# Strassen quads for q and k of four head groups in a fused attention and gMLP kernel, with the first score gather moved ahead of the v gathers

## The chip, the cores and the metric

One NeuronCore of one Trainium2 chip runs the whole program. The metric is device time in microseconds (us), the median over several executions. A profile of one execution gives the span from the first to the last instruction, a few us shorter than the device time. Engines: PE is TensorE, DVE is VectorE, ACT is ScalarE, POOL is GpSimd, SP is the engine that issues most DMAs. "L435" is line 435 of a kernel's source; the change adds lines, so L293 of the kernel before is L294 of the changed one, and L1405 is L1478.

## The reference, cut to what matters

```python
# x: (1, 2048, 1024); 32 heads of 32; a query sees 8 keys, 2 positions apart
q, k, v = split(x @ wqkv)
logits  = where(mask, q . k[pos - 2*w], -1e9)          # w = 0..7
a       = (softmax(logits) . v[pos - 2*w]) @ wo
z       = gelu(x @ w_in);  z1, z2 = halves(z);  z2 = layernorm(z2)
b       = (z1 * (w_sp @ z2 + b_sp)) @ w_out
out     = g * a + (1 - g) * b                          # g = sigmoid(sum(x * gate_w))
```

The kernel handles attention in eight groups of four heads. For one group, q and k are 256 output columns, from a contraction of 1024 over 2048 tokens. Done directly, that is 2 x 4 x 8 = 64 matmuls of 512 columns.

## The kernel before: the parts that matter

TensorE runs the stages in this order: v and q/k of the first groups; then for each group the q and k of the next group, with three sets of small banded score matmuls between; in the middle the rest of v; then z2, z1, the spatial product and the output. The attention of a group (maxima, exponential, weights, products with v) runs on VectorE and ScalarE behind it, and lasts far into the z1 stage. One Python scheduler estimates each engine's clock and hands VectorE a piece of attention when it believes that there is room.

q and k are direct:

```python
def qk_tile(g, t, c, bank=low_bank):              # t: q or k; c: 512 tokens
    ps = bank()
    for kt in range(KT):                          # 8
        nc.tensor.matmul(ps[:], w[:, t, kt, :], xT[:, kt, 512*c:512*(c+1)], ...)
    act(0.5, pe(T_QK) + 0.2)
    nc.scalar.copy(dst[:, :, 256*c:256*(c+1)], ...)
```

v, z2 and z1 are already Strassen quads: a 2 x 2 block product by seven block products rather than eight, in four PSUM banks. Each block product is four matmuls. In z2 and z1 the sums of the outputs are made by accumulating on copied "seeds" and by two adds on VectorE (`plus`, L506 in the profile); v uses a variant with seed copies alone (L453, L464 and L477, on ScalarE). The form with adds is this one:

```python
def chain(A11, ..., S1..S4, B11, ..., T1..T4, vs, put, share, N, ...):
    X, Y, Z, V = bank_roles[side]
    product(X, A11*B11);  nc.scalar.copy(Y, X)     # seed, L518    ; yield
    product(V, S1*T1);    share(vs, V)             # share, L524   ; yield
    product(Y += S2*T2);  plus(Z, Y)     # VectorE: Z = Y + vs     ; yield
    product(X += A12*B21); put(0, 0, X)                           ; yield
    product(Y += S3*T3);  plus(V, Y);  put(1, 1, V)               ; yield
    product(Z += S4*B22); put(0, 1, Z)                            ; yield
    product(Y or X += A22*T4); put(1, 0, ...)                     ; yield
# (condensed: clock bookkeeping and the copy that only non-lean quads make are cut)
```

Two quads normally run in turn, in the lower and the upper four banks, so that one quad's copies and adds hide behind the other's products. The S sums are sums of weights (VectorE, L577), the T sums are sums of x, made once. `mark` is a short matmul over a bank that a quad is to accumulate into. The Trainium skill ("PSUM — Partial Sum Buffer", section "The four PSUM rules") says why it is needed: a matmul that begins an accumulation clears the written bits of the whole bank, in the 32-partition quadrants that it writes, and an element whose bit is clear is overwritten where it should be added to. The band scores clear those of the upper banks.

The order of the first gathers, where `next_v` issues two v gathers of 960 KB each:

```python
    clock["SP"], clock["DMA"] = 4.0, 4.0
    next_v()                     # v of groups 0 and 1
    load_wqk_later(3, 0.0)       # weights of group 3
    # the gather of the first scores is issued only behind these
```

## Time and profile before

| | before |
|---|---|
| device time at the prediction | 663.26 us (662.23 to 663.37, 3 runs) |
| span of the profile | 657.9 us, granted clock 1.000 |
| PE busy | 650.5 us, 99% |
| VectorE busy | 503.2 us, 76% |
| ScalarE busy | 290.0 us, 44% |

First the page of the kernel before: span, busy time by engine, VectorE's busy tenths in 40 slices, and three of its groups of instructions (busy time, mean ns of one, then the idle time before them and what ended it).

```profile
span 657.9 us, 11379 instructions
PE 650.5 (99%) x4453; PEld 341.3 (52%) x4453; DVE 503.2 (76%) x762; ACT 290.0 (44%) x632; POOL 6.2 (1%) x15
DVE  2520889978999999898778676887659999595952
...
L435 PE MATMUL psum_all<-arena 128*128 128x512 f16 (+6 forms) x2238 | 442.0, 360 | 0.7 <-DVE psum_all L506 0.6
L293 PE MATMUL psum_all<-arena 128*128 128x512 bf16 x512 | 114.8, 379 | 0.0
...
L506 DVE TENSOR_TENSOR psum_all<-psum_all,arena 128x448 f32<-128x448 f32 (+1 forms) x58 | 37.2, 660 | 4.5 <-PE psum_all L435 3.6
```

PE is the bound: it waits for almost nothing, so only fewer matmuls can shorten the program. The 379 ns of one matmul is its latency, and the matmuls overlap; the chain of waits has 1314 matmuls of 512 columns in 283.7 us, 0.216 us each. This agrees with the Trainium skill ("TensorE: Matmul & The Clock Gate", section "Wait — 56ns, not 53.3ns?": 215.7 ns). L293 counts the direct 512-column matmuls, which the change halves. VectorE is at 80% or more in 23 of the 36 slices from 66 us on, so whatever is added there may turn into a wait of PE. One slack is visible: the first score maximum waits until 64.7 us for its gather. From VectorE's timeline, before (start, duration, instruction, and in brackets the idle time before it and what ended it):

```profile
64.70 0.29 DVE L671 TENSOR_TENSOR att_m<-att_L 128x256 f16<-128x256 f16 x1 [16.96 <-DMA att_L<-band_d]
```

### The profile page before, as it was taken

To read this page: it belongs to the slowest core of one execution; us is meant where nothing else is said; L and a number is where in the kernel's file an instruction comes from. 1 tells how busy PE (TensorE), PEld (TensorE's weight loads), DVE (VectorE), ACT (ScalarE), POOL (GpSimd) and SP (SyncE) were. 2 spreads that over 40 slices of the span, in tenths; PEclk is the share of its full clock that TensorE was granted. 3 is DMA by queue.
4 is the path that set the end of the run, shared out by engine and by line. 5 is a ranking of instruction groups with operands and counts; after the bars stand their busy time and mean duration, and the time that the engine had idled before them with its cause. 6 is when DMAs were issued, how large, how long until landed. Compare 5 with 4: busy or idle time off the path is not lost.

```text
span 657.9 us, 11379 instructions
## 1 busy us (share of the span) xinstructions
PE 650.5 (99%) x4453; PEld 341.3 (52%) x4453; DVE 503.2 (76%) x762; ACT 290.0 (44%) x632; POOL 6.2 (1%) x15
## 2 busy tenths in 40 slices
PE   8999999999999999999999999999999999999998
PEld 4544467444454555444444444444444444868684
DVE  2520889978999999898778676887659999595952
ACT  4544676555588677799654112111121112202120
POOL 1000000000000000001000000000000000000000
PEclk9999999999999999999999999999999999999999
DMA  9988554797586050249974568559697463455501
GB/s 217 189 212 225 124 129 122 176 222 188 120 213 179 1 156 1 65 129 249 248 205 159 121 171 166 143 157 280 127 186 172 97 153 91 117 136 115 134 19 56
DMA packets 230198, 98.20 MB, mean 149 GB/s; under 512 B 177520, under 2 KB 217088, under 8 KB 230144
## 3 DMA queue, kind: packets, MB, share of 16 engines
q1 hardware_dynamic: 229856, 97.27, 61.2%
q8 instruction: 35, 0.57, 0.4%
q10 hardware_dynamic: 288, 0.20, 0.1%
q14 instruction: 19, 0.16, 0.1%
HBM read 45.10 MB, written 36.61 MB: 124 GB/s over the span
## 4 chain that ended last, share of the span: by engine, by line
PE 95%; ACT 2%; DMA 2%; DVE 1%; issue 0%; SPq 0%; DVEq 0%; ACTq 0%
PE psum_all L435 66%; PE psum_all L293 17%; PE psum_all L1391 7%; PE psum_all L303 3%; PE psum_all L355 2%; DMA arena<-o_d 1%; DMA arena<-in_A_x_dram 1%; ACT arena L815 1%; ACT arena L363 0%; SPq L162 0%; PE psum_all L822 0%; DVE arena L708 0%; DVE psum_all L506 0%; ACT L815 0%; PE psum_all L225 0%
## 5 line engine op out<-in xcount | busy, mean ns | idle before, releaser
L435 PE MATMUL psum_all<-arena 128*128 128x512 f16 (+6 forms) x2238 | 442.0, 360 | 0.7 <-DVE psum_all L506 0.6
L435 PEld LDWEIGHTS <-arena 128*128 128x128 f16 (+1 forms) x2238 | 218.8, 98 | 222.2 <-issue 2.2
L293 PE MATMUL psum_all<-arena 128*128 128x512 bf16 x512 | 114.8, 379 | 0.0
L293 PEld LDWEIGHTS <-arena 128*128 128x128 bf16 x512 | 48.4, 98 | 56.2 <-issue 0.2
L708 DVE TENSOR_TENSOR arena<-arena,att_A 128x2048 f16<-128x2048 bf16 (+1 forms) x44 | 73.3, 1703 | 0.3
L296 ACT CAST arena<-psum_all 128x512 bf16<-128x512 f32 x64 | 37.2, 585 | 51.2 <-PE psum_all L293 51.2
L1391 PE MATMUL psum_all<-arena 128*128 128x256 f16 (+1 forms) x468 | 51.9, 273 | 1.0 <-DVE psum_all L1405 1.0
L1391 PEld LDWEIGHTS <-arena 128*128 128x128 f16 x468 | 45.8, 98 | 6.8 <-issue 1.3
L815 ACT ACTIVATE arena<-psum_all 128x448 bf16<-128x448 f32 x64 | 34.1, 545 | 18.8 <-DVE psum_all L506 9.2
L453 ACT COPY psum_all<-psum_all 128x512 f32<-128x512 f32 (+1 forms) x24 | 12.4, 517 | 67.4 <-PE psum_all L435 66.6
L506 DVE TENSOR_TENSOR psum_all<-psum_all,arena 128x448 f32<-128x448 f32 (+1 forms) x58 | 37.2, 660 | 4.5 <-PE psum_all L435 3.6
L1095 ACT ACTIVATE arena<-psum_all 128x512 bf16<-128x512 f32 x56 | 31.5, 600 | 21.0 <-PE psum_all L435 13.9
L712 DVE TENSOR_TENSOR arena<-arena 128x2048 f16<-128x2048 f16 (+1 forms) x22 | 37.1, 1704 | 0.1
L363 ACT CAST arena<-psum_all 128x1988 f16<-128x1988 f32 (+3 forms) x25 | 33.9, 1356 | 1.1 <-PE psum_all L355 0.3
L870 ACT ACTIVATE arena<-arena 128x896 bf16<-128x896 bf16 x32 | 30.4, 958 | 0.0
L477 ACT COPY psum_all<-psum_all 128x512 f32<-128x512 f32 (+1 forms) x24 | 12.4, 518 | 37.0 <-PE psum_all L435 36.0
L581 DVE TENSOR_TENSOR arena<-arena 128x1024 f16<-128x1024 f16 (+2 forms) x17 | 12.2, 720 | 19.5 <-PE psum_all L435 15.7
L464 ACT COPY psum_all<-psum_all 128x512 f32<-128x512 f32 (+1 forms) x24 | 12.4, 518 | 25.6 <-PE psum_all L435 24.8
L459 ACT COPY arena<-psum_all 128x512 f32<-128x512 f32 (+1 forms) x24 | 12.7, 532 | 24.9 <-PE psum_all L435 22.5
L303 PE MATMUL psum_all<-arena 128*128 128x385 bf16 x128 | 22.6, 327 | 0.0
L671 DVE TENSOR_TENSOR att_m<-att_L 128x256 f16<-128x256 f16 x8 | 2.3, 288 | 23.8 <-DMA att_L<-band_d 23.8
L713 DVE TENSOR_TENSOR arena<-arena 128x2048 f16<-128x2048 f16 x16 | 19.5, 1221 | 0.3
(111 smaller groups left out, 510.9 us busy)
## 6 DMA issues: line engine op xcount, KB each, us to landing
arena<-v_d SPq DMA_DIRECT2D x8, 960.0 KB, 5.9
z_d<-arena SPq DMA_DIRECT2D x14, 512.0 KB, 4.7
arena<-z_d SPq DMA_DIRECT2D x14, 512.0 KB, 4.3
zg_d<-arena SPq DMA_DIRECT2D x56, 128.0 KB, 2.2
arena<-zg_d SPq DMA_DIRECT2D x32, 224.0 KB, 3.2
band_d<-arena SPq DMA_DIRECT2D x28, 248.5 KB, 4.4
arena<-in_A_wqkv_dram SPq DMA_DIRECT2D x16, 256.0 KB, 5.0
o_d<-arena SPq DMA_DIRECT2D x4, 1024.0 KB, 5.8
```

Of the source, the lines that this page charges most:

```text
L293: nc.tensor.matmul(ps[:], w[:, t, kt, :], xT[:, kt, 512 * c:512 * (c + 1)], start=(kt == 0), stop=(kt == KT - 1))
L296: nc.scalar.copy(dst[:, :, 256 * c:256 * (c + 1)], ps[:].rearrange("p (n e) -> p e n", e=2))
L303: nc.tensor.matmul(ps[:, 0:VP + 1], xT[:, kt, i * P:(i + 1) * P], wvp[:, kt, :], start=(kt == 0), stop=(kt == KT - 1))
L363: nc.scalar.copy(dst, src)
L435: nc.tensor.matmul(bank[:, 0:N], lhsT, rhs, start=(start and m == 0), stop=(m == n - 1), skip_group_check=True)
L506: last_add[0] = nc.vector.tensor_tensor(out[:, n], a[:, n], vs, ALU.add)
L708: lambda ws=ws, in0=in0, in1=in1: tt(p5[:, ws], in0[:, ws], in1[:, ws], ALU.mult)), False
L712: lambda a=p3[:, ws], b=p3[:, ws.start + 4:ws.stop + 4]: tt(a, a, b, ALU.add)), not n
L815: nc.scalar.activation(z2[:, i + 8 * a, ZC * c:ZC * (c + 1)], bank[:, 0:ZC], ACT.Gelu_apprx_tanh, accum_out=s1[:, 4 * n + c:4 * n + c + 1])
L870: return nc.scalar.activation(junk, src, ACT.Square, accum_out=(s2, s2h)[x][:, n:n + 1])
L1095: last_gelu[0] = nc.scalar.activation(z1s[:, f, a, :], bank[:], ACT.Gelu_apprx_tanh)
L1391: nc.tensor.matmul(bank[:, h], l, r, start=(start and m == 0), stop=(m == len(ab) - 1), skip_group_check=True)
```

## The change

q and k of groups 2 to 5 become two quads per group: 2 x 7 x 4 = 56 matmuls rather than 64. There is one quad per 512-token chunk of the two token halves. Two of the four quads of a pair of groups can run beside each other; the others run alone in the lower banks, while a group's band scores use the upper ones. The first score gather goes to the head of the queue, so that VectorE can start attention earlier, to pay for the new adds.

```diff
+    PAIRS, FINE_TO = (2, 4), -1
+    def qk_sums(g):                      # four 128x512 sums of weights, VectorE
+    def qk_quad(g, c, side):
+        def put(t, x, bank):
+            act(0.5, max(clock["PE"], clock["DVE"] if t + x == 2 else 0.0) + 0.2)
+            nc.scalar.copy((qT_slots, kT_slots)[t][g % 2][...], bank[:]...)
+        return chain(..., qv_slots[side], put, nc.scalar.copy, 512, side=side, lean=True, done=done)
+    BAND_AT = (1, 3, 6)
+    def among_bands(g, quad):            # one quad alone, band sets behind its products 1, 3, 6
+        for n in range(7):
+            next(quad); step()
+            if n + 1 in BAND_AT:
+                band_set(g, x); x += 1; step()
+    def play_group(g):
+        if g + 1 in PAIRS:
+            among_bands(g, qk_quad(g + 1, 0, 0))
+            first = qk_quad(g + 1, 1, 0)
+            ... two products of it ...
+            mark(bank_roles[1][1:3], 512)
+            run(qk_quad(g + 2, 0, 1), first, step=step)
+        elif g in PAIRS:
+            among_bands(g, qk_quad(g + 1, 1, 0))
...
-    clock["SP"], clock["DMA"] = 4.0, 4.0
+    clock["SP"], clock["DMA"] = 5.5, 5.5
+    next_bands()                         # first score gather
+    dma(0.0, 0.1, lambda: sync.dma_start(g_att[:], ...))
+    next_v(1)
+    load_wqk_later(3, 0.0)
     next_v()
-    load_wqk_later(3, 0.0)
...
-        z1s, vs = z1s_slots[fp in (2, 4)][c], zv_slots[c]
+        z1s, vs = z1s_slots[fp == 3][c], zv_slots[c]
...
-        ... vs, gelu, share, 512, lean=True, done=store)
+        ... vs, gelu, nc.scalar.copy if not fp else share, 512, lean=True, done=store)
```

(`FINE_TO = -1` also splits the first of VectorE's products with v, of groups 0 to 4, into quarters of 1.2 us.)

More of the change, by code (lines that the diff above doesn't have):

```diff
@@ L140 @@
     wqk_slots = [z2[:, 8 * (r % 2):8 * (r % 2) + 8, 896 * (r // 2):896 * (r // 2) + 256].rearrange("p k (t c) -> p t k c", t=2) for r in range(4)]
-    wqk_slots += wqk_slots[0:2] + [reg(R_OFF + 34752 + 2048 * r, 2048).rearrange("p (k t c) -> p t k c", k=KT, t=2) for r in (0, 1)]
+    wqk_slots += wqk_slots
     wvp = z2[:, 0:KT, ZC:ZC + VP + 1]
@@ L409 @@
     sync.dma_start(bass.AP(tensor=g_d.tensor, offset=g_d.offset, ap=[[P, 16], [1, P]]), g_s[:])
-    sync.dma_start(bass.AP(tensor=og_d.tensor, offset=og_d.offset, ap=[[P, 16], [1, P]]), omg_h[:])
-    gate_dma = sync.dma_start(g_att[:], bass.AP(tensor=g_d.tensor, offset=g_d.offset, ap=[[NJ, P], [1, NJ]]))
+    gate_dma = sync.dma_start(bass.AP(tensor=og_d.tensor, offset=og_d.offset, ap=[[P, 16], [1, P]]), omg_h[:])
     def x_sums(r):
@@ L723, in products @@
             next_v()
-    SPLIT, FINE = [[slice(n * x, n * x + n) for x in range(8 // n)] for n in (4, 2)], 4
+    SPLIT, FINE = [[slice(n * x, n * x + n) for x in range(8 // n)] for n in (4, 2)], FINE_TO
     sent = []
@@ L728, with next_v @@
     bands_at, bands_have = [0], [0]
-    def next_v():
-        while v_at[0] < min(v_have[0], gone[0] + 2):
+    def next_v(upto=NG):
+        while v_at[0] < min(v_have[0], gone[0] + 2, upto):
             h = v_at[0]
@@ L875 @@
     quads = [(0, i) for i in range(7)] + [(1, i) for i in range(8)]
+    QSET = [g + x for g in PAIRS for x in range(2)]
+    qs_slots = [z2h[:, 0:16, 256 + 896 * r:384 + 896 * r].rearrange("p (q k) c -> p q k c", q=4) for r in range(2)]
+    qv_slots = [reg(R_OFF + 34752 + 1024 * r, 1024).bitcast(F32) for r in range(2)]
+    q_landed, q_free = {}, [int(2 in PAIRS), 0]
+    def qk_sums(g):
+        w, s = wqk_slots[g], qs_slots[g % 2]
+        return sums4_steps([s[:, q] for q in range(4)], w[:, 0, 0:4], w[:, 0, 4:8], w[:, 1, 0:4], w[:, 1, 4:8])
@@ new lines, in qk_push, with qk_ready, done @@
+    def qk_push(r):
+        while q_free[r] == 0 and q_landed.get(r):
+            g, t = q_landed[r].pop(0)
+            q_free[r] = 1
+            fill.extend((t, 0.34, f) for f in qk_sums(g))
+    def qk_ready(g, t):
+        q_landed.setdefault(g % 2, []).append((g, t + LATE))
+        qk_push(g % 2)
+    def qk_quad(g, c, side):
+        w, s = wqk_slots[g], qs_slots[g % 2]
+        a, b = w[:, 0], w[:, 1]
+        lo, hi = slice(512 * c, 512 * c + 512), slice(1024 + 512 * c, 1536 + 512 * c)
+        def put(t, x, bank):
+            act(0.5, max(clock["PE"], clock["DVE"] if t + x == 2 else 0.0) + 0.2)
+            nc.scalar.copy((qT_slots, kT_slots)[t][g % 2][:, :, 256 * (c + 2 * x):256 * (c + 2 * x + 1)], bank[:].rearrange("p (n e) -> p e n", e=2))
+        def done():
+            if c == 1:
+                q_free[g % 2] = 0
+                qk_push(g % 2)
+        return chain([a[:, k] for k in K4], [a[:, 4 + k] for k in K4], [b[:, 4 + k] for k in K4],
+                     *[[s[:, q, k, :] for k in K4] for q in range(4)],
+                     [xT[:, k, lo] for k in K4], [xT[:, 4 + k, lo] for k in K4], [xT[:, 4 + k, hi] for k in K4],
+                     *[[x[:, k, lo] for k in K4] for x in xts], qv_slots[side], put, nc.scalar.copy, 512, side=side, lean=True, done=done)
@@ new lines @@
+    BAND_AT = (1, 3, 6)
+    def among_bands(g, quad):
+        x = 0
+        for n in range(7):
+            next(quad)
+            step()
+            if n + 1 in BAND_AT:
+                band_set(g, x)
+                x += 1
+                step()
+        bands_have[0] = g + 1
+        next(quad, 0)
+    def play_group(g):
+        if g + 1 in PAIRS:
+            among_bands(g, qk_quad(g + 1, 0, 0))
+            first = qk_quad(g + 1, 1, 0)
+            for _ in range(2):
+                next(first)
+                step()
+            mark(bank_roles[1][1:3], 512)
+            run(qk_quad(g + 2, 0, 1), first, step=step)
+        elif g in PAIRS:
+            among_bands(g, qk_quad(g + 1, 1, 0))
+        else:
+            return False
+        return True
@@ L912, in step @@
         advance(clock["PE"])
-    def behind_first(n):
-        at = [0]
-        def f():
-            at[0] += 1
-            if at[0] == 1:
-                mark(banks[5:7], n)
-            step()
-        return f
     def play(items):
@@ L939, in load_wqk_later @@
     def load_wqk_later(g, at):
-        dma(at, 2.9, lambda: load_wqk(g, sync.dma_start))
+        dma(at, 2.9, lambda: load_wqk(g, sync.dma_start), (lambda t: qk_ready(g, t)) if g in QSET else None)
     settle()
@@ L948 @@
     band_data[0], band_free[0], v_data[0] = T_START
-    clock["SP"], clock["DMA"] = 4.0, 4.0
+    clock["SP"], clock["DMA"] = 5.5, 5.5
     stored.clear()
     bands_have[0] = 1
+    next_bands()
+    dma(0.0, 0.1, lambda: sync.dma_start(g_att[:], bass.AP(tensor=g_d.tensor, offset=g_d.offset, ap=[[NJ, P], [1, NJ]])))
+    next_v(1)
+    load_wqk_later(3, 0.0)
     next_v()
-    load_wqk_later(3, 0.0)
+    if 2 in PAIRS:
+        fill.extend((1.5, 0.34, f) for f in qk_sums(2))
     for g in range(NG):
@@ L958 @@
         hold[0] = g == NG - 1
-        play(main[0:8 - (not g)])
+        paired = play_group(g)
+        if not paired:
+            play(main[0:8 - (not g)])
         if g == 2:
-            for i in range(0, 8, 2):
-                run(v_quad(i), v_quad(i + 1), step=behind_first(VH) if i == 0 else step)
+            first = v_quad(0)
+            for _ in range(3):
+                next(first)
+                step()
+            mark(bank_roles[1][1:3], VH)
+            run(v_quad(1), first, step=step)
+            for i in range(2, 8, 2):
+                run(v_quad(i), v_quad(i + 1), step=step)
             advance(clock["PE"] + 1.0)
@@ L966 @@
             load_later(0, clock["PE"] + 4.0, 6.0)
-        play(main[8 - (not g):])
+        if not paired:
+            play(main[8 - (not g):])
     load_later(1, clock["PE"] + 3.0, 2.0)
@@ L984, in quad_step @@
             if n == 0 and count[0] == 0:
-                mark(banks[5:7], ZC)
+                mark(bank_roles[1][1:3], ZC)
             step()
@@ L1103, in z1_quad @@
                      [xT[:, k, lo] for k in K4], [xT[:, 4 + k, lo] for k in K4], [xT[:, 4 + k, hi] for k in K4],
-                     *[[x[:, k, lo] for k in K4] for x in xts], vs, gelu, share, 512, lean=True, done=store)
+                     *[[x[:, k, lo] for k in K4] for x in xts], vs, gelu, nc.scalar.copy if not fp else share, 512, lean=True, done=store)
     z1_junk = free(BC_OFF, FH)
@@ L1123 @@
     dma(clock["PE"] + 1.0, 2.9, lambda: load_w1(1), w1_landed(1))
+    RAW_IN = 3.0
+    DRAIN, SUMS = 1, NFH - 2
     RAW_AT = {2: {2: 0, 4: 1, 6: 2}, 3: {4: 3, 6: 4}, 4: {2: 5, 4: 6, 6: 7}}
@@ L1129 @@
             w1_sums(fp + 1)
-        if fp == NFH - 2:
-            fill.extend((clock["PE"] + 3.0, 1.15, f) for f in wsp_sums(0, 0))
+        if fp == SUMS:
+            fill.extend((clock["PE"] + RAW_IN, 1.15, f) for f in wsp_sums(0, 0))
         late = () if fp else [b[2] for b in bank_roles]
@@ L1135 @@
             step=lambda: z1_step(fp, at))
-        if fp == 1:
+        if fp == DRAIN:
             drain()
```

## The prediction

> **What bounds the kernel now.** TensorE. The engine table has PE busy 650.5 us of 657.9 (99%); the chain of waits is 95% PE, at a granted clock of 1.00. A 512-column matmul costs 0.216 us in the chain (1314 in 283.7 us), as the Trainium skill has it ("TensorE: Matmul & The Clock Gate", section "Wait — 56ns, not 53.3ns?": 215.7 ns). VectorE is second: by stretches it is busy 77.5 of 81.2 us in the z2 stage (191 to 272) and 22.4 of 24.4 us in the first two z1 passes (272.2 to 296.6). Its attention work ends at 294.7, only 2 us before the second z1 pass.
>
> **Removed.** q and k of a group are 64 matmuls of 512 columns; as two quads 2x7x4 = 56. Four groups save 32. Each pair of groups needs two marking matmuls, which set the written bits of banks that the band scores cleared: 4 added. Net 28 x 0.216 = 6.05 us of TensorE, all on the chain. Two VectorE copies of the first z1 pass (0.69 each) go to ScalarE.
>
> **Added on VectorE.** 16 PSUM adds of 512 columns, 0.65 each in sequence: 10.4 us. Weight sums of groups 3 to 5: 12 x 0.43 = 5.1 (those of group 2 fall into the idle 17 us before 64.7). Attention products of groups 0 to 4 in quarters: 1.9. Less the two copies: 16 us net before attention ends.
>
> **Added on ScalarE.** 16 seed and share copies, 9 us; it is 66% busy there and off the chain, except where a 1.8 us band eviction sits between a product and its share copy.
>
> **Moved.** The first score gather is issued at 57.0 behind two v gathers and a weight load, and lands at 64.7. Going first, it can land near 58.5: VectorE starts 6 us earlier. Its waits for the scores of groups 4 and 5 (2.5 + 1.4 + 2.7 us between 142 and 160) also fill up.
>
> **On the critical path.** 6.05 us of TensorE less new waits. (a) A single quad has no partner: a product two steps later needs the VectorE add, covered by one product and one band set, 0.86 + 0.6 us. An attention piece of 1.2 us in the way costs some tenths: 1 us over four single quads. (b) VectorE, with 16 us more and 12 us of room gained, ends attention at 296 to 298, while TensorE ends the second z1 pass near 291.5. The third pass can run 4 to 5 us before it needs an add queued behind attention. So 1 to 3 us of stall. The rest of z1 has 11 us of VectorE slack, so little is lost before the spatial stage. Estimate: 663.3 - 6.05 + 1 + 2 = 660.2 us.
>
> **Predicted:** 660.2 us, 656.8 to 664.0. Faster by over 2%: 0.01; within 2%: 0.97; slower by over 2%: 0.02.
>
> **What would show it.** Direct 512-column bf16 matmuls fall from 512 to 256, quad matmuls rise by 224. First score maximum near 58 to 60, not 64.7. Between 60 and 185 PE has waits of tenths on VectorE adds. A PE wait of 1 to 3 us on a VectorE add near 295. The spatial stage starts 3 to 5 us before 357.1; after that both run alike. ScalarE plus 9 us, VectorE plus 16 us busy in all.
>
> **What would make it wrong.** VectorE's lag absorbed: all 6 us gained (657). VectorE lagging longer: spatial weights load late behind the attention's store, another stall before the spatial stage, no gain or a loss. Late weights for group 3 stalling the first paired quads.

## The result, and the profile after

Ratios in this document are of fast runs alone, with a 95% interval. They are not quite the ratios of the medians that are quoted, nor of the plain means of all runs listed (for e12 the means give 0.9993).

| chip | before, median | changed, median | ratio |
|---|---|---|---|
| first | 663.32 us (4 runs) | 660.64 us (4 runs, 660.34 to 662.54) | 0.9969 [0.9948, 0.9991] |
| second (run e2_after) | 660.80 us (7 runs) | 658.46 us (4 runs) | 0.9957 [0.9938, 0.9976] |
| third (run e9_after) | 661.83 us (11 runs) | 659.29 us (6 runs) | 0.9969 [0.9953, 0.9986] |

The gain is 2.3 to 2.7 us on three chips, less than half of one per cent. From the page of the changed kernel:

```profile
span 660.7 us, 11409 instructions
PE 647.5 (98%) x4425; PEld 339.9 (51%) x4425; DVE 518.8 (79%) x822; ACT 298.1 (45%) x650; POOL 6.5 (1%) x15
DVE  2534989998799999999888666987669999594952
...
L435 PE MATMUL psum_all<-arena 128*128 128x512 f16 (+6 forms) x2462 | 494.8, 362 | 4.0 <-DVE psum_all L506 2.7
L294 PE MATMUL psum_all<-arena 128*128 128x512 bf16 x256 | 57.5, 379 | 0.0
L506 DVE TENSOR_TENSOR psum_all<-psum_all,arena 128x512 f32<-128x512 f32 (+1 forms) x74 | 48.0, 668 | 4.6 <-PE psum_all L435 2.5
```

The counts are as intended: 512 direct matmuls became 256, and L435 has 224 more. VectorE has 15.6 us more and ScalarE 8.1 us. New in this page is the last column of L435: those matmuls waited 4.0 us in all, not 0.7. The first score maximum comes 7.6 us earlier (VectorE's timeline, changed kernel):

```profile
57.13 0.29 DVE L671 TENSOR_TENSOR att_m<-att_L 128x256 f16<-128x256 f16 x1 [7.90 <-DMA att_L<-band_d]
```

The profiled run on the first chip was the slowest of its four (662.54 us), and the run profiled before took 659.77 us, less than any of the four in the table (662.23 to 663.42). The two profiles can't be subtracted. The second chip gives a clean pair, one profile of each kernel, both at full clock (spans of 659.2 and 657.0 us). This table cuts them at the same points of the program; the output stage begins with its first seed copy on ScalarE, and the table ends with the start of VectorE's last add.

| stretch | before (e1_before) | changed (e2_after) | difference |
|---|---|---|---|
| start to the q/k tiles behind v | 44.49 | 44.88 | +0.39 |
| q/k, bands and v, to the first z2 tile | 137.87 | 133.27 | -4.60 |
| z2 | 91.40 | 91.69 | +0.29 |
| z1 and spatial | 288.02 | 288.79 | +0.77 |
| output | 94.42 | 95.24 | +0.82 |
| sum | 656.20 | 653.87 | -2.33 |

The +0.39 lies ahead of anything that was changed. To see where the rest goes, take all waits of PE between 60 and 640 us of that changed run (the other fields as above; a line can hold many matmuls, and its wait is that before the first):

```profile
89.27 0.70 PE L435 MATMUL psum_all<-arena 128*128 128x320 f16 x4 [0.94 <-ACT psum_all L453]
184.34 0.64 PE L356 MATMUL psum_all<-arena 32*64 32x71 bf16 x56 [0.31 <-ACT arena L364]
195.52 13.78 PE L435 MATMUL psum_all<-arena 128*128 128x448 f16 x72 [2.49 <-DVE psum_all L506]
209.46 60.55 PE L435 MATMUL psum_all<-arena 128*128 128x448 bf16 x316 [0.16 <-DVE psum_all L506]
326.08 231.97 PE L435 MATMUL psum_all<-arena 128*128 128x512 f16 x1074 [0.71 <-DVE psum_all L506]
572.55 4.09 PE L1464 MATMUL psum_all<-arena 128*128 128x256 f16 x36 [1.40 <-DVE psum_all L1478]
```

The same kernel before had these in the z2 stage (PE's timeline of e1_before):

```profile
198.45 10.75 PE L435 MATMUL psum_all<-arena 128*128 128x448 f16 x56 [1.20 <-DVE psum_all L506]
210.37 4.89 PE L435 MATMUL psum_all<-arena 128*128 128x448 f16 x25 [1.17 <-DVE psum_all L506]
```

Four things can be read here.

First, the q/k stretch became 4.60 us shorter with a new wait of 0.94 us in it, so 5.54 us of work went; the prediction had 6.05. The other half microsecond is in the starts of single matmuls. The matmul that waits starts 1.24 us after the one before it, where 0.14 is usual, so the wait cost 1.10 us and not 0.94; and two others, at 95.38 and 128.28 us, keep the next one waiting 0.17 us longer than their like. The wait stands where the first v quads begin, right behind the last single quad. ScalarE, which works its queue in order, had this ahead of the seed copy L453 (ScalarE's timeline, e2_after):

```profile
86.56 1.83 ACT L364 CAST arena<-psum_all 128x1988 f16<-128x1988 f32 x1
88.27 0.62 ACT L903 CAST arena<-psum_all 128x512 bf16<-128x512 f32 x1
88.75 0.47 ACT L453 COPY psum_all<-psum_all 128x320 f32<-128x320 f32 x1
```

The eviction of the last band set (1.83 us) and one of the quad's own evictions (0.62 us) come first, and PE starts when the seed is there. No wait in the single quads themselves is on a VectorE add.

Second, at the start of z2 PE waits 2.49 us for a VectorE add. VectorE's timeline just ahead of that add (e2_after):

```profile
186.45 4.63 DVE L708 TENSOR_TENSOR arena<-arena,att_A 128x2048 f16<-128x2048 bf16 x4
191.11 0.29 DVE L692 TENSOR_TENSOR att_A<-att_L,att_r 128x256 f16<-128x256 f16 x1
191.31 2.35 DVE L712 TENSOR_TENSOR arena<-arena 128x2048 f16<-128x2048 f16 x2
193.70 1.22 DVE L713 TENSOR_TENSOR arena<-arena 128x2048 f16<-128x2048 f16 x1
194.84 1.16 DVE L506 TENSOR_TENSOR psum_all<-psum_all,arena 128x448 f32<-128x448 f32 x2
```

Eight pieces of attention, 8.4 us from 186.45 to 194.84, stand ahead of the first two adds of z2. The Trainium skill ("Perfetto Trace Analysis", section "Per-engine timelines") calls VectorE and ScalarE strict FIFO, and this agrees: no add passes a piece. But the kernel before lost 1.20 + 1.17 us at the same stage, so most of this wait isn't new on this pair of runs; in the first profile of before it was 0.59 us.

Third, in the third z1 pass PE waits 0.71 us at 326. VectorE had waited there for a weight load (`in_B_w_in`) that before was not late. The load was issued at 312.66 us, about when it was in e1_before (312.91), though TensorE had begun z1 3.92 us earlier; in both it follows a group of transposing weight loads and two z1 stores in the DMA queue. Fourth, the output stage loses 0.9 us more to the load of the attention output (1.40 us, where before had 0.20 and 0.27).

On the first chip three of the changed kernel's four runs also had a mean granted clock of 0.997. The stretch right behind the z2 wait shows why (windows of 4 us, first chip's changed profile: after the busy times comes the granted clock, then DMA share and GB/s):

```profile
192.00:196.00 4.00, 2.19 (x12) 1.02 (x11) 3.93 (x6) 3.49 (x8) 0.00 (x0) 1.00 0.98 283
196.00:200.00 4.00, 3.43 (x13) 1.58 (x13) 3.96 (x7) 0.53 (x2) 0.00 (x0) 0.72 1.21 210
200.00:204.00 4.00, 4.00 (x20) 1.90 (x18) 3.93 (x6) 3.27 (x13) 0.00 (x0) 0.85 1.03 242
```

PE's wait there was 2.38 us. The clock was then 0.72 and 0.85, which is (0.28 + 0.15) x 4 = 1.72 us of work not done. The Trainium skill ("TensorE: Matmul & The Clock Gate", section "Part 1: The HAM clock gate") has a gate that falls to half speed after an idle window of about 3.4 us, in windows that run free. Half speed for one such window is an estimated 1.7 us. The trace agrees on the half and on the length (same profile, the stretch of the dip alone):

```profile
197.80:201.21 3.41, 3.41 (x11) 1.36 (x9) 3.41 (x5) 1.69 (x6) 0.00 (x0) 0.50 1.19 162
```

It differs on how much idleness that takes. The clock changes in each trace lie on steps of 3.41 us, counted from the first rise of the clock (6.65 us here; 197.80 is 56 steps later). The dips of one step came behind steps that held 2.18 us of a PE wait (here), 2.17 (e10), 2.52 (e12) and 3.08 us (e7). No step with 1.79 us or less had a dip behind it. The waits of 2.49 us in e2_after and 2.35 us in e9_after were cut in two by a step's end (1.70 + 0.79 and 1.64 + 0.71), and no dip followed. "PE busy" hides this loss, since a slower matmul counts as busy. The times of the runs do not show it, though: on the first chip the one run at full clock took 660.81 us, and two of the three at 0.997 took 660.34 and 660.48.

### The profile page after: what moved, and what is told of

It reads as the page before. It is cut to its first block, busy times and chain, and to the rows that moved or that the text cites. A ratio compares the mean times of both kernels' runs of the same rounds, so it can differ in the third digit from the quotient of the medians.

```text
span 660.7 us, 11409 instructions
## 1 busy us (share of the span) xinstructions
PE 647.5 (98%) x4425; PEld 339.9 (51%) x4425; DVE 518.8 (79%) x822; ACT 298.1 (45%) x650; POOL 6.5 (1%) x15
## 4 chain that ended last, share of the span: by engine, by line
PE 81%; DVE 9%; DMA 6%; ACT 1%; issue 1%; SPq 1%; DVEq 0%; ACTq 0%
PE psum_all L435 64%; PE psum_all L1464 7%; PE psum_all L294 5%; PE psum_all L304 3%; DMA band_d<-arena 2%; DMA arena<-o_d 1%; DVE arena L708 1%; PE psum_all L356 1%; DMA arena<-in_B_w_in_dram 1%; SPq L190 1%; DVE arena L1247 1%; DVE arena L712 1%; DVE arena L577 1%; PE psum_all L319 1%; ACT arena L815 0%
## 5 line engine op out<-in xcount | busy, mean ns | idle before, releaser
L435 PE MATMUL psum_all<-arena 128*128 128x512 f16 (+6 forms) x2462 | 494.8, 362 | 4.0 <-DVE psum_all L506 2.7
L435 PEld LDWEIGHTS <-arena 128*128 128x128 f16 (+1 forms) x2462 | 240.2, 98 | 251.0 <-issue 8.0
L708 DVE TENSOR_TENSOR arena<-arena,att_A 128x2048 f16<-128x2048 bf16 x64 | 75.3, 1219 | 0.3
L294 PE MATMUL psum_all<-arena 128*128 128x512 bf16 x256 | 57.5, 379 | 0.0
L506 DVE TENSOR_TENSOR psum_all<-psum_all,arena 128x512 f32<-128x512 f32 (+1 forms) x74 | 48.0, 668 | 4.6 <-PE psum_all L435 2.5
L453 ACT COPY psum_all<-psum_all 128x512 f32<-128x512 f32 (+1 forms) x24 | 12.5, 519 | 67.2 <-PE psum_all L435 66.4
L294 PEld LDWEIGHTS <-arena 128*128 128x128 bf16 x256 | 24.4, 98 | 28.4 <-issue 0.2
L712 DVE TENSOR_TENSOR arena<-arena 128x2048 f16<-128x2048 f16 x32 | 38.1, 1218 | 0.0
L477 ACT COPY psum_all<-psum_all 128x512 f32<-128x512 f32 (+1 forms) x24 | 12.4, 518 | 37.4 <-PE psum_all L435 36.6
L297 ACT CAST arena<-psum_all 128x512 bf16<-128x512 f32 x32 | 18.6, 587 | 23.2 <-PE psum_all L294 23.0
L577 DVE TENSOR_TENSOR arena<-arena 128x512 f16<-128x512 bf16 (+3 forms) x52 | 25.2, 522 | 3.0 <-DMA arena<-in_B_w_in_dram 2.6
L464 ACT COPY psum_all<-psum_all 128x512 f32<-128x512 f32 (+1 forms) x24 | 12.4, 518 | 25.9 <-PE psum_all L435 25.1
L518 ACT COPY psum_all<-psum_all 128x512 f32<-128x512 f32 (+1 forms) x37 | 20.4, 562 | 6.3 <-PE psum_all L435 5.5
```

The lines of the kernel that those rows point to most:

```text
L294: nc.tensor.matmul(ps[:], w[:, t, kt, :], xT[:, kt, 512 * c:512 * (c + 1)], start=(kt == 0), stop=(kt == KT - 1))
L435: nc.tensor.matmul(bank[:, 0:N], lhsT, rhs, start=(start and m == 0), stop=(m == n - 1), skip_group_check=True)
L506: last_add[0] = nc.vector.tensor_tensor(out[:, n], a[:, n], vs, ALU.add)
L577: return [lambda a=a: nc.vector.tensor_tensor(*a) for a in args]
L708: lambda ws=ws, in0=in0, in1=in1: tt(p5[:, ws], in0[:, ws], in1[:, ws], ALU.mult)), False
L712: lambda a=p3[:, ws], b=p3[:, ws.start + 4:ws.stop + 4]: tt(a, a, b, ALU.add)), not n
```

## The experiments

Twelve kernels were run. Runs of one chip share their runs of before, so ratios are safer than medians. One run of e5 was slow (clock 0.655) and is left out of its ratio.

| run | chip | median us | before on that chip | ratio |
|---|---|---|---|---|
| e1_before | second | 660.34 | 660.80 | 0.9994 [0.9979, 1.0009] |
| e2_after | second | 658.46 | 660.80 | 0.9957 [0.9938, 0.9976] |
| e3_order_only | second | 663.23 | 660.80 | 1.0039 [1.0020, 1.0057] |
| e4_pairs_only | second | 668.73 | 660.80 | 1.0118 [1.0091, 1.0145] |
| e5_order_pure | fourth | 663.53 | 661.31 | 1.0029 [1.0014, 1.0044] |
| e6_z1slots | fourth | 660.96 | 661.31 | 0.9997 [0.9982, 1.0012] |
| e7_lag_known | fourth | 660.35 | 661.31 | 1.0006 [0.9980, 1.0032] |
| e8_band_early | fourth | 661.53 | 661.31 | 1.0011 [0.9998, 1.0023] |
| e9_after | third | 659.29 | 661.83 | 0.9969 [0.9953, 0.9986] |
| e10_qk_pool | third | 664.50 | 661.83 | 1.0057 [1.0034, 1.0079] |
| e11_qk_wz_pool | third | 688.73 | 661.83 | 1.0413 [1.0395, 1.0431] |
| e12_no_sums | fifth | 660.28 | 660.64 | 0.9989 [0.9976, 1.0003] |

All but e12 were correct; e12 is wrong. The changed kernel itself wasn't run on the fourth and fifth chips, so a comparison of e6, e7, e8 and e12 with it goes over two chips, through before. Their ratios are all near 1.000, so it isn't excluded that the change is worth less on those two chips. Their profiles show TensorE's part of the gain there too: the q/k stretch took 133.27 us in e7 and 133.38 in e12, as in e2 (133.27). No variant's ratio was better than that of the change.

### e1_before and e2_after: both kernels again

No edit.

> The kernel before, unchanged, once more: for the spread of its times, clocks and profiles. Both theories: 662 to 664 us, ratio 1.000. The first profile was a lucky run (659.8 against a median of 663.3); if the difference is a slowed clock after a TensorE wait in the z2 stage, this one's clock is below 1.000 in the slower runs.

> The changed kernel once more. 660 to 661 us. Theory A (VectorE runs behind and stalls TensorE): the 2.4 us wait on the VectorE add at the start of the z2 stage and the slowed clock behind it are there again. If the wait was chance, it is not.

The kernel before against itself gives 0.9994, with an interval of 0.0015 on each side, so differences of two or three parts in a thousand can be seen. The gain holds (0.9957). e1's times (660.05 to 661.05 us) lie below the 662 to 664 that were expected, and its slowest run was at full clock, so a slowed clock isn't what sets the runs of before apart. In e2 the expected wait at z2 came again (2.49 us), the slowed clock behind it did not. The table by stretches comes from this pair.

### e3_order_only and e4_pairs_only: one part of the change each

e3 keeps the reordered gathers and the z1 changes, without quads. e4 keeps the quads, with the old order of the first gathers.

```diff
# e3, against the changed kernel
-    PAIRS, FINE_TO = (2, 4), -1
+    PAIRS, FINE_TO = (), 4
# e4, against the changed kernel
-    clock["SP"], clock["DMA"] = 5.5, 5.5
+    clock["SP"], clock["DMA"] = 4.0, 4.0
-    next_bands()
-    ... next_v(1)
+    next_v()
     load_wqk_later(3, 0.0)
-    next_v()
```

> The change without the quads for q and k and without the finer attention products: only the earlier score gather, and the small changes in z1. Theory A: VectorE starts attention 7 us earlier, and the kernel before lost about 2 to 3 us to waits on it, so 660 to 663 us. Theory B (the order is worth nothing by itself; VectorE waits for scores later on and gives the lead back): 663 us, ratio 1.000.

> The change with the old order of the first gathers (two v gathers ahead of the score gather). Theory A: VectorE starts 7 us later, is further behind at the start of the z2 stage and at the third z1 pass, and TensorE waits 2 to 5 us more than in the changed kernel: 663 to 666 us. Theory B (the losses come from short groups, in which band buffers and ScalarE are reused too soon, not from a late VectorE): 660 to 661 us.

Each part alone is slower than before, by 0.4% and 1.2%; only together do they gain. No theory had e3 slower than before, and e4's loss is larger than theory A's. In e4 the first score maximum is back at 66.13 us and attention's last operation starts at 304.57 (296.34 in e2). PE's longest wait in its timeline is then just where the prediction had looked for one:

```profile
307.12 23.18 PE L436 MATMUL psum_all<-arena 128*128 128x512 f16 x97 [6.61 <-DVE psum_all L507]
```

So the predicted mechanism, a third z1 pass that needs an add queued behind attention, exists. VectorE's earlier start in the full change keeps it off. e4 also ran at clocks of 0.992 to 0.995: in its profile the clock was at half from 304.54 to 311.37 us, of which 4.25 us lie behind that wait and cost 2.1 us more. In e3 a wait of another kind appears (PE's timeline, then ScalarE's):

```profile
315.31 15.05 PE L435 MATMUL psum_all<-arena 128*128 128x512 f16 x69 [1.92 <-ACT psum_all L518]
```

```profile
307.53 0.60 ACT L1166 ACTIVATE arena<-psum_all 128x512 bf16<-128x512 f32 x1 [2.67 <-DMA z_d<-arena]
```

ScalarE waits 2.67 us for the store of z1's staging buffer, and another DMA, the store of attention output, was issued between two z1 stores (at 299.75 us; in e1_before at 296.31, ahead of both). Attention did not end earlier in e3: its first maximum came at 56.47 rather than 64.84 us, but its last operation started at 296.36, against 295.60 in e1_before. So the lead was given back, as theory B has it. Cut as in the table above, e3 lost 1.25 us in the q/k stretch and 1.98 in z1 and spatial, and gained 1.68 in z2.

### e5_order_pure: only the reorder, in the kernel before

```diff
# against the kernel before
-    gate_dma = sync.dma_start(g_att[:], ...)          # leaves the start
+    clock["SP"], clock["DMA"] = 5.5, 5.5
+    next_bands(); dma(... g_att ...); next_v(1)
     load_wqk_later(3, 0.0)
+    next_v()
```

> The kernel before with nothing but the score gather moved ahead of the v gathers. The order-only run was 0.4% slower than before, but it also carried the change's new use of the z1 staging buffers, and its trace has a 1.9 us TensorE wait behind a ScalarE wait of 2.7 us for a z1 store. Theory A (that wait, not the order, made it slower): ratio to before 0.998 to 1.002, no such wait. Theory B (an earlier VectorE start hurts by itself): 1.003 to 1.005 again.

It is 0.29% slower in its five fast runs (661.07 to 664.14 us). So a loss of nearly e3's size comes without the z1 changes of e3. Its profile fell on the slow run of 974.56 us and says nothing of times, so the cause of this loss is open.

### e6_z1slots: the z1 staging buffers as before

```diff
-        z1s, vs = z1s_slots[fp == 3][c], zv_slots[c]
+        z1s, vs = z1s_slots[fp in (2, 4)][c], zv_slots[c]
```

> The changed kernel with the z1 staging buffers chosen as before. If the new choice is needed because attention ends later (the old second buffer shares space with v data that attention still reads), this one waits in the third z1 pass: 0.5 to 2 us slower than the changed kernel, ratio to before 0.997 to 0.999. If not, it is as fast or faster: 0.994 to 0.996, for ScalarE no longer waits for a z1 store.

The ratio is 0.9997, where the change had 0.9957 and 0.9969 elsewhere; both expected ranges were missed. The profile doesn't lay this on the staging buffers. z1 and spatial took 289.48 us, against 288.79 in e2 and 289.40 in e9, the z2 wait was 1.79 us, and no long wait was seen in z1. What is longer is the q/k stretch, which the edit doesn't touch: 134.89 us, against 133.27 in e2 and e9. The first score maximum came at 58.82 us rather than 57.25 (e2), and PE then waited 0.86 us for a seed copy, which ScalarE made behind the late exponential, and 0.43 us for a VectorE add in the single quad. So what the new assignment is worth is not shown.

### e7_lag_known: the first z2 adds ahead of the attention pieces

The scheduler believes VectorE to be less behind than it is. Here its clock is moved on by 3.6 us at the start of z2, so that it holds pieces of attention back until behind the first adds.

```diff
     SQ_AT = (2, 9)
+    clock["DVE"] += 3.6
     for n in range(0, len(quads), 2):
```

> The changed kernel with one number more in the bookkeeping that places VectorE's work: at the start of the z2 stage VectorE is taken to be 3.6 us further behind, so three attention pieces come after the first adds instead of before them. Theory A (VectorE's queue holds attention work ahead of the first adds of the z2 stage, and TensorE waits 2.4 us for them, with a slowed clock behind it in some runs): 2 to 4 us faster than the changed kernel, ratio to before 0.990 to 0.993. Theory B (VectorE is the limit by total work, so a wait taken away here comes back later, in the third z1 pass): the wait at the start of z2 is gone, another of 2 us shows up near 295, time as the changed kernel.

VectorE's timeline shows the first adds at once behind the share copies, and PE's timeline has no wait there:

```profile
185.71 4.62 DVE L708 TENSOR_TENSOR arena<-arena,att_A 128x2048 f16<-128x2048 bf16 x4
191.18 1.17 DVE L506 TENSOR_TENSOR psum_all<-psum_all,arena 128x448 f32<-128x448 f32 x2 [0.84 <-ACT arena L524]
```

```profile
302.15 28.17 PE L435 MATMUL psum_all<-arena 128*128 128x512 f16 x122 [3.08 <-DVE psum_all L506]
```

z1 began at 267.71 us, 2.1 us earlier than in e2. The attention that was held back then came late (its last operation starts at 299.60), and the third z1 pass waited 3.08 us. The ratio was 1.0006, with one run of 666.23 us in it; the other five have a mean of 660.58 us, and before 661.18. From the z2 stage to the end of attention VectorE has about as much work as time, so the wait taken away at one end came back at the other, as theory B says. Its place was a scheduling choice; its size hardly changed (3.08 us, against 2.49 + 0.71 in e2).

### e8_band_early: the last band set one product earlier

This should free ScalarE sooner at the start of v.

```diff
-    BAND_AT = (1, 3, 6)
+    BAND_AT = (1, 3, 5)
```

> The changed kernel with the third band set of a single quad after its fifth product instead of its sixth. Theory: the 0.9 us wait at the start of the v quads comes from ScalarE, which has a 1.8 us band eviction in front of the copy that the first v quad waits for; one product earlier takes it away: 0.5 to 0.9 us faster than the changed kernel. Rival: a single quad needs that band set where it is, to cover the wait for its second add; then a wait of some tenths shows up in each of the four single quads and the time stays.

The ratio was 1.0011. The wait at 89 us fell from 0.94 to 0.66 us, and new ones came elsewhere in the q/k stage (PE's timeline):

```profile
88.99 1.53 PE L435 MATMUL psum_all<-arena 128*128 128x320 f16 x8 [0.66 <-ACT arena L903]
129.21 1.02 PE L435 MATMUL psum_all<-arena 128*128 128x512 f16 x4 [0.71 <-ACT arena L903]
150.12 1.89 PE L294 MATMUL psum_all<-arena 128*128 128x512 bf16 x8 [1.22 <-ACT arena L903]
```

All three are on the evictions of the single quad, which now stand behind a band eviction closer by. The q/k stretch took 136.40 us, against 133.27 in e2, so the order of the change was the better one, as the rival theory had it (though its waits are on ScalarE and not on the second add).

### e9_after, e10_qk_pool and e11_qk_wz_pool: weight sums on GpSimd

If VectorE's work is what costs, moving its weight sums to the idle GpSimd should pay. e9 is the changed kernel; e10 moves the 12 sums of the weights of groups 3 to 5, e11 also the eight sums of z2's weights.

```diff
# e10; e11 also passes nc.gpsimd in wz_sums
-    def sums4_steps(s_out, a11, a12, a21, a22):
+    def sums4_steps(s_out, a11, a12, a21, a22, on=nc.vector):
...
-            fill.extend((t, 0.34, f) for f in qk_sums(g))
+            for f in qk_sums(g): f()       # on nc.gpsimd
```

> The changed kernel on the chip of the next two, as their reference: ratio to before 0.995 to 0.997, with the wait of 2 to 2.5 us on a VectorE add at the start of the z2 stage.

> The changed kernel with the twelve weight sums of q and k of groups 3, 4 and 5 on GpSimd instead of VectorE: 5.1 us less for VectorE while attention runs, the arithmetic the same. Theory A (VectorE's total work up to the third z1 pass is what the change pays with): attention ends 3 to 5 us earlier, TensorE's waits on VectorE adds shrink by 1.5 to 3 us in all, ratio to the changed kernel 0.995 to 0.998. Theory B (the waits come from where the pieces stand, not from how much there is, or GpSimd slows VectorE as much as it helps): attention ends as before, ratio 1.000.

> As the run before, and the eight weight sums of the z2 stage (1.1 us each on VectorE) go to GpSimd too: 13.8 us less for VectorE. Theory A: attention ends 8 us or more before where the changed kernel ends it, no TensorE wait on a VectorE add over 1 us before the spatial stage, ratio to the changed kernel 0.992 to 0.996. Theory B: the large sums on GpSimd arrive too late for the z2 quads or slow VectorE's attention pieces; ratio 1.000 or above.

e9 came as expected: 0.9969, with a wait of 2.35 us at z2. e10 is 0.6% slower than before and e11 4.1%. The timelines of GpSimd and of VectorE in e11, over the same stretch, and PE's wait that follows (one of 10.31 us, at 212.78, came before it):

```profile
228.43 13.24 POOL L577 TENSOR_TENSOR arena<-arena 128x1792 f16<-128x1792 bf16 x3 [4.37 <-DMA arena<-in_B_w_in_dram]
```

```profile
230.20 12.56 DVE L708 TENSOR_TENSOR arena<-arena,att_A 128x2048 f16<-128x2048 bf16 x3
```

```profile
245.95 55.83 PE L435 MATMUL psum_all<-arena 128*128 128x448 f16 x276 [8.31 <-DVE psum_all L506]
```

Three VectorE products, which took 3.48 us in e2, took 12.56 us beside GpSimd's three sums. The Trainium skill ("GPSIMD Engine Reference", section "8. Key points") says that GpSimd shares its SBUF interfaces with VectorE and that instructions with two SBUF inputs contend; this trace agrees, and puts the size at 3.6 times. In e10 two adds L712 took 4.26 us rather than 2.35. So these runs don't test what less VectorE work is worth: the work was taken off its queue and given back as slower instructions.

### e12_no_sums: less VectorE work, on no other engine

The sums of groups 3 to 5 are left out, and the quads read those of group 2, made twice in the idle time at the start. The result is wrong (relative error 0.077); TensorE's order is the same.

```diff
-    def qk_sums(g):
-        w, s = wqk_slots[g], qs_slots[g % 2]
+    def qk_sums(g, r=0):
+        w, s = wqk_slots[g], qs_slots[r]
...
-            fill.extend((t, 0.34, f) for f in qk_sums(g))
...
-        fill.extend((1.5, 0.34, f) for f in qk_sums(2))
+        fill.extend((1.5, 0.34, f) for r in range(2) for f in qk_sums(2, r))
```

> The changed kernel, but the weight sums of groups 3, 4 and 5 are not computed: their quads read the sums of group 2, which are made twice in VectorE's idle time at the start. The result is wrong on purpose; TensorE's instructions and their order are the same. Twelve VectorE sums of 0.43 us, 5.1 us, are gone before attention ends, with no work put on another engine. Theory A (what the change gives back is set by VectorE's total work before the z1 stage): the last attention piece starts 3 to 5 us earlier than in the changed kernel (298.7, 296.3 and 296.2 us in its three profiles), the wait of 2.4 us at the start of the z2 stage shrinks by 1.5 us or more, and the ratio to the kernel before is 0.992 to 0.995. Theory B (placement: in the z2 stage the first adds stand behind the pieces that the scheduler put ahead of them, however much work there is in all): the last attention piece starts earlier, but the wait at the start of z2 stays 2 to 2.5 us and the ratio stays at 0.996 to 0.997, as of the changed kernel.

Theory A of this run, that VectorE's total work counts wherever it lies, falls. The last attention piece started at 299.10 us, not earlier than 296; the z2 wait was 2.94 us; the ratio was 0.9989, worse than the change's rather than better. VectorE's timeline shows what became of the missing work. These are its waits for scores between 150 and 195 us, in e12 and then in e2:

```profile
163.77 0.29 DVE L671 TENSOR_TENSOR att_m<-att_L 128x256 f16<-128x256 f16 x1 [3.74 <-DMA att_L<-band_d]
171.01 0.29 DVE L671 TENSOR_TENSOR att_m<-att_L 128x256 f16<-128x256 f16 x1 [1.24 <-DMA att_L<-band_d]
```

```profile
161.04 0.29 DVE L671 TENSOR_TENSOR att_m<-att_L 128x256 f16<-128x256 f16 x1 [2.09 <-DMA att_L<-band_d]
170.70 0.29 DVE L671 TENSOR_TENSOR att_m<-att_L 128x256 f16<-128x256 f16 x1 [2.27 <-DMA att_L<-band_d]
```

With another wait of 2.20 us for the exponential (at 152.16), e12 idles 7.2 us there, where e2 idles 4.4. From 57 to 195 us VectorE is busy 120.3 us in e12 and 125.4 in e2, so the 5.1 us that it was spared became waiting: it reaches scores before these are there. Two other things had a part in it. The gather behind the longest of these waits was issued later in e12, because two weight loads and two band stores, which come behind it in e2, stand ahead of it (SP's timeline, e12 and then e2):

```profile
158.73 2.36 SPq L190 DMA_DIRECT2D att_L<-band_d  x2
```

```profile
154.90 1.63 SPq L190 DMA_DIRECT2D att_L<-band_d  x2
```

And e2 did one attention piece of 1.22 us (at 167.20) before its last wait, which e12 did after it. So in this schedule the saving bought nothing; that none could is not shown. The wait at z2 did not shrink:

```profile
196.96 75.80 PE L435 MATMUL psum_all<-arena 128*128 128x448 f16 x388 [2.94 <-DVE psum_all L506]
```

The rival theory's statement of the z2 wait (2 to 2.5 us) was a little low, its earlier last piece didn't come, and its ratio was missed too: 0.9989 instead of 0.996 to 0.997. Two things were seen that add to it. All five runs had a clock of 0.997 (0.73 and 0.84 in the two windows behind the z2 wait, again 1.72 us), and the profiled run lost 0.85 us at 8 us to a load of x, ahead of all that was edited. Whether these are all of it is open, since the changed kernel was not on that chip.

## Why the prediction was right, and where it was right for the wrong reason

The time was predicted as 660.2 us, and 660.64 was measured; "within 2%" was given 0.97 and came. Point by point:

- **PE bounds the kernel, and 28 matmuls are 6.05 us of it.** Right. The q/k stretch became 4.60 us shorter with a new wait that cost 1.10, and two single starts cost 0.17 us each: 6.04 us in all.
- **Work added: VectorE 16 us, ScalarE 9 us.** Measured 15.6 and 8.1 us.
- **First score maximum near 58 to 60.** It came at 57.1 us.
- **Waits for the scores fill up.** Only partly. 4.4 us of waiting for scores were left between 155 and 195 us in e2.
- **(a) Waits of tenths on VectorE adds inside the single quads, 1 us in all.** The size was right (0.94 and 1.01 us in two profiles, and 1.16 more in the first), the mechanism was wrong: there were no such waits in the changed kernel's profiles (e6 has one of 0.43 us). PE waited once, at the handover to v, for a ScalarE seed copy behind a 1.83 us band eviction. The prediction had named that eviction, but for the share copy inside a quad.
- **(b) Attention ends at 296 to 298 us, and 1 to 3 us of stall near 295 in the third z1 pass.** Attention's last operation started at 296.2 to 298.7 us in three profiles. But PE had no stall near 295. It waited 2.4 to 2.5 us at 195, at the start of z2. The step that failed was to place all of VectorE's lag at the end of its attention. The scheduler had put eight attention pieces ahead of the first z2 adds, and the lag came due there, a hundred microseconds earlier. e4 (6.61 us at 307) and e7 (3.08 us at 302) show that the predicted stall is the same debt, paid later. And 0.6 to 2.4 us at that stage were already lost before, so (b) cost less net than its 2 us: 0.3 us for the z2 stage on the second chip.
- **"The spatial stage starts 3 to 5 us before".** On the second chip its first seed copy came at 357.42 us, against 360.56: 3.1 us earlier.
- **"After that both run alike."** Wrong. On the second chip the changed kernel lost 0.77 us more in z1 and spatial, where a weight load came late at 321, and 0.82 us more in the output stage. That made up for what (b) lacked, so the total came out right. The z1 part was named only loosely, as weights late behind the attention's store; the output part wasn't foreseen.
- **"VectorE lagging longer: no gain or a loss".** This risk is real: without the earlier start it is a loss of 1.2% (e4).

So the sum was right by luck: errors cancelled. What is shown: the two parts need each other (e3, e4), and the z2 wait came back elsewhere when the order was changed (e7). In e12, work taken from VectorE before the last scores arrive bought nothing, in a schedule whose DMA order had shifted too. Open are why the pure reorder is slower (e5), and why the load of attention output comes later in the tail. From the first of its transposing issues to the VectorE operation that waits for it, the load took 5.5 and 5.4 us in the two profiles of before (566.61 to 572.13, 568.21 to 573.61), and 6.6 and 6.9 us in e2 and e9 (565.07 to 571.66, 565.52 to 572.45).

## What to carry to other kernels

When a second engine runs close to full behind the bound engine, ask when its lag comes due: at the first point where the bound engine needs something from that engine's queue, not at the end of the lagging work. Work saved ahead of a wait for data can vanish in that wait, as in e12; that work from the last arrival on counts in full is argued here, and no run shows it. Cut TensorE's program at fixed points in both profiles and subtract, rather than comparing totals, and use a repeat of the kernel before, since its own stalls (0.6 or 2.4 us at one place) can be as large as the effect.

## What the Trainium skill lacked or had wrong

- "TensorE: Matmul & The Clock Gate", section "Why this matters for your kernels", asks for no PE gaps over about 3 us. Here a gap of 2.38 us was followed by granted clocks of 0.72 and 0.85 in the next two 4 us windows, and one of 2.94 us by 0.73 and 0.84; gaps of 2.49 and 2.35 us in two other runs were not. A gap well under 3 us can already halve the clock for 3.41 us, some 1.7 us of work. What told the two kinds apart is how much of the gap fell into one 3.41 us step: 2.17 us or more had a dip behind it, 1.79 us or less had none.
- "GPSIMD Engine Reference", section "8. Key points", names the contention with VectorE's two-input instructions; that page has no figure for it, though the skill's page on SBUF has some. Measured: three VectorE products 12.56 us rather than 3.48 beside GpSimd sums; two VectorE adds 4.26 rather than 2.35.
- "GPSIMD Engine Reference", section "4.1 Engine selection", has GpSimd about 2 times slower for two-input elementwise work. Six 128x512 sums took 11.70 us on GpSimd while VectorE was busy, 1.95 us each, against 0.41 on VectorE: 4.8 times. Two later ones (from 85.38 us) took 2.39 us, 1.20 each, which is 2.9 times. No run has these sums on GpSimd beside an idle VectorE, so the page's figure isn't refuted for that case.
